# Attention values of the wide tiles by halves, in three of the gates' PSUM banks and beside the next half's scores

## Chip, cores and metric

One core of a Trainium2 chip. The metric is the device time in microseconds of one execution, median of several.

## The reference

Sliding-window causal attention over 8 batches and 8 heads (576 positions, head size 64, window 64), followed by a gated feed-forward layer without biases on the 4608 tokens of 512 features:

```python
rel = pos[:, None] - pos[None, :]
mask = (rel >= 0) & (rel < 64)
scores = np.where(mask, 0.125 * q @ k.T, -1e9)     # per batch and head
attn = softmax(scores) @ v
x = attn.transpose(0, 2, 1, 3).reshape(4608, 512)
out = (np.maximum(x @ w_gate, 0) * (x @ w_val)) @ w_out   # 512 -> 1536 -> 512
```

Inputs and output are float32; the kernel computes its products in float16 with float32 sums.

## The kernel before

The tokens are worked in ten tiles: four of 384 tokens (tiles 0 to 3), then six of 512 (tiles 4 to 9, the wide ones). The stage of tile t does the feed-forward layer of tile t on TensorE, and beside it, woven in, the attention of tile t+1.

The feed-forward part of a wide stage is `hidden` and `output`. `hidden` makes 12 pairs of tiles of 128 hidden features by 512 tokens: four products with w_gate (h0), four with w_val (h1), each group into one PSUM bank of the pool f_ps. ScalarE takes relu of h0 (`relu`, L453) and VectorE multiplies it with h1 (`gate`, L456) into g_sb. `output` then makes four output tiles of 128 tokens, twelve products each (`out_mm`, L482), also in a bank of f_ps; ScalarE copies each out (`out_evac`, L489) and SP stores it. The twelfth product of the first output tile needs the last gate.

The attention part of a wide tile works on two quads of four 64-token windows. `q_st` makes the 64 score products of a quad (L233: keys as weights, 32 rows by 128 columns of the array, 64 columns moving) into two tiles of two banks of the pool a_ps. `q_exp` (ScalarE, L352, four per quad) and `q_mask` (VectorE, L356, four per quad) make the probabilities pw. `t_pv` makes the 128 value products of both quads at once (L371: pw as weights, 128 rows by 32 columns, 65 columns moving: 64 values and the sum of the probabilities). `t_recip` and `t_norm` (VectorE, L386, L391) divide by the sums, and `t_turn` (L396) transposes into xt, the input of the next stage. A bank holds seven 32-token slices of values (BS = 7); the sixteen slices of a tile and four heads lie as 7, 7 and 2, the twos of both head groups in a bank of f_ps, the rest in all four banks of a_ps.

PSUM has eight banks: f_ps four of one bank (tag h: h0, h1, output tiles, and the rest of the values), a_ps two of two banks (scores and values).

The order of instructions is set by a planner, the Weaver. It counts the time of the large products in a clock of its own, and holds a heap of small pieces with due times: before each group of large products (in `output` before each product) it issues the pieces that are due. A piece may advance the clock by what it returns (0.72 for `q_st`, 1.25 for `t_pv`). `ahead(t)` plans the attention of tile t+1 from the clock T at the start of stage t; `plan_wide` sets its pieces. Each engine works through its own queue in the order issued.

The loads of q, k and v, and the copies that spread v to windows that overlap (`v_spread`), are issued by POOL; v is held for two batches, and a load of v waits until the values that last read its slot are made (`v_load`, L191). Transposes of q and k (`qk_trans`, L185) are on VectorE, and `wide_loads` sets their times.

Of the kernel before, what the change touches and what calls it, by code (L numbers as in the profile page):

```python
# [10 lines left out]
FP32 = mybir.dt.float32  # L11
FP16 = mybir.dt.float16
ACT = mybir.ActivationFunctionType
MUL = mybir.AluOpType.mult
# [30 lines left out]
def kernel(  # L45
# [10 lines left out]
    nc = tc.nc  # L56
    B, H, S, D = q.shape
# [8 lines left out]
    G = 4  # L66
# [3 lines left out]
    NS = 4  # L70
    NL = (NT - NS * TT) // WT
# [8 lines left out]
    a_n = ctx.enter_context(tc.tile_pool(name="a_n", bufs=2))  # L80
# [12 lines left out]
    NG = S // 64  # L93
    VW = D + 2
    v16s = [persist.tile([128, NG, H, VW], FP16, name=f"v16_{i}") for i in range(2)]
# [34 lines left out]
    W = Weaver()  # L130
# [4 lines left out]
    def xt_tile(t):  # L135
        if t not in xts:
            xts[t] = x_sb.tile([128, NC, WT], FP16, name="xt")
        return xts[t]
# [75 lines left out]
    def one_bank(name):  # L214
        return f_ps.tile([128, 512], FP32, name=name, tag="h")

    def two_banks(name):
        return a_ps.tile([128, 2, 512], FP32, name=name, tag="a")
# [10 lines left out]
    def st_block(to, g, hh, n, biased=False):  # L229

        b, w = divmod(n, NG)
        rows = slice(32 * g, 32 * g + 32)
        return [lambda dh=dh: nc.tensor.matmul(  # L233
            to, kTs[b % 2][rows, hh, 64 * w:64 * w + 128, dh], qTs[b % 2][rows, hh, 64 * w:64 * w + 64, dh],
            start=(dh == 0 and not biased), stop=(dh == 1), skip_group_check=biased) for dh in range(2)]

    def run_rows(rows):

        for step in zip(*rows):
            for dh in range(2):  # L240
                for block in step:
                    block[dh]()
# [89 lines left out]
    QW = 4  # L332
    WS = 2 * WT // 64
    BS = 512 // VW
    quads = {}
    wides = {}

    def q_window(qd, i):
        return NS * TT // 64 + QW * qd + i

    def q_st(qd):

        halves = [two_banks("st") for _ in range(2)]
        d = quads[qd] = {"st": [halves[g // 2][:, g % 2] for g in range(G)], "p": [None] * G}
        run_rows([[st_block(d["st"][g][:, 256 * hh + 64 * i:256 * hh + 64 * i + 64], g, hh, q_window(qd, i))
                   for hh in range(2) for i in range(QW)] for g in range(G)])
        return 0.72

    def q_exp(qd, g):
        d = quads[qd]  # L350
        d["p"][g] = a_p.tile([128, 2 * QW, 64], FP16, name="pw")
        nc.scalar.activation(d["p"][g].rearrange("p n c -> p (n c)"), d["st"][g], ACT.Exp, scale=scale)  # L352

    def q_mask(qd, g):
        p = quads[qd]["p"][g]
        nc.vector.tensor_tensor(p, p, mask[:, None, :].to_broadcast([128, 2 * QW, 64]), MUL)  # L356

    def t_pv(t):

        d = wides[t] = {"pv": [two_banks("pv") for _ in range(2)], "rest": one_bank("pv"),  # L360
                        "x": a_n.tile([128, 2, WS, 2, D // 2], FP16, name="xw"), "r": a_n.tile([128, 2, WS, 1], FP32, name="rw")}
        for qh in range(2):
            qd = 2 * (t - NS) + qh
            for hh in range(2):
                for i in range(QW):
                    b, vw = divmod(q_window(qd, i), NG)
                    for s in range(2):
                        n = 2 * (QW * qh + i) + s
                        to = d["pv"][hh][:, n // BS, VW * (n % BS):] if n < 2 * BS else d["rest"][:, VW * (2 * hh + n - 2 * BS):]
                        for j in range(G):  # L370
                            nc.tensor.matmul(to[32 * j:32 * j + 32, 0:D + 1],  # L371
                                             quads[qd]["p"][j][:, QW * hh + i, 32 * s:32 * s + 32],
                                             v16s[b % 2][:, vw, G * hh + j, 0:D + 1],
                                             start=True, stop=True, skip_group_check=True)
        return 1.25

    def t_parts(d, hh):

        rest = d["rest"][:, 0:4 * VW].rearrange("p (a s c) -> p a s c", a=2, c=VW)
        return [(d["pv"][hh][:, k, 0:BS * VW].rearrange("p (s c) -> p s c", c=VW), BS * k, BS * k + BS) for k in range(2)] + [  # L380
            (rest[:, hh], 2 * BS, WS)]

    def t_recip(t, hh):
        d = wides[t]
        for pv, s0, s1 in t_parts(d, hh):
            nc.vector.reciprocal(d["r"][:, hh, s0:s1], pv[:, :, D:D + 1])  # L386

    def t_norm(t, hh, k):
        d = wides[t]
        pv, s0, s1 = t_parts(d, hh)[k]  # L390
        nc.vector.tensor_tensor(d["x"][:, hh, s0:s1], pv[:, :, 0:D].rearrange("p s (c e) -> p s e c", e=2),  # L391
                                d["r"][:, hh, s0:s1, :, None].to_broadcast([128, s1 - s0, 2, D // 2]), MUL)

    def t_turn(t, hh):
        dst = xt_tile(t)[:, 2 * hh:2 * hh + 2].rearrange("p e (s c) -> p s e c", c=32)
        nc.vector.transpose(dst, wides[t]["x"][:, hh])  # L396
        if hh == 1:
            normed[0] = t

    def plan_wide(t, TA, TB, P):  # L400
        for qd, T in ((2 * (t - NS), TA), (2 * (t - NS) + 1, TB)):
            W.at(T, lambda qd=qd: q_st(qd))
            for g in range(G):
                W.at(T + 0.8 + 0.55 * g, lambda qd=qd, g=g: q_exp(qd, g))
                W.at(T + 1.35 + 0.55 * g, lambda qd=qd, g=g: q_mask(qd, g))
        W.at(P, lambda: t_pv(t))
        for hh in range(2):
            W.at(P + 0.7 + 3.0 * hh, lambda hh=hh: t_recip(t, hh))
            for i, k in enumerate((2, 0, 1)):
                W.at(P + 1.0 + 3.0 * hh + 0.5 * i, lambda hh=hh, k=k: t_norm(t, hh, k))  # L410
            W.at(P + 2.4 + 3.0 * hh, lambda hh=hh: t_turn(t, hh))

    def plan_batch(b, load, trans):
        for i, (name, hh) in enumerate((n, hh) for n in "kq" for hh in range(2)):
# [115 lines left out]
    with tc.manual_schedule():  # L530
# [78 lines left out]
        def pair(t, TA, TB, P):  # L609
            for u, T in ((2 * t, TA), (2 * t + 1, TB)):  # L610
                W.at(T, lambda u=u: u_st(u))
                plan_exps(T, u)
            W.at(P, lambda: u_pv(2 * t) + u_pv(2 * t + 1))
            for n in range(2):
                u = 2 * t + n
                W.at(P + 0.7 + 1.7 * n, lambda u=u: u_recip(u))
                for hh in range(2):
                    W.at(P + 0.9 + 0.5 * hh + 1.7 * n, lambda u=u, hh=hh: u_norm(u, hh))
                W.at(P + 1.9 + 1.7 * n, lambda u=u: u_turn(u))
# [12 lines left out]
        def wide_loads(t, T):  # L632
            w0 = q_window(2 * (t - NS), 0)
            b = (w0 + 2 * QW - 1) // NG
            us = list(range(UB * b, UB * b + UB)) if w0 <= NG * b else []
            if t == NS:
                us.insert(0, UB * b - 1)
            if w0 <= NG * b:
                plan_batch(b, T - 12.0, (T, T + 1.4, T + 2.8, T + 4.2))
            for u in us:  # L640
                W.at(T - 6.0, lambda u=u: v_load(u))
                W.at(T + 1.0, lambda u=u: v_spread(u, pool))

        def ahead(t):
            T = W.clock
            if t + 1 < NS:
                pair(t + 1, T + 11.0, T + 14.0, T + 17.5)
            elif t + 1 == NS:
                plan_wide(t + 1, T + 9.5, T + 13.0, T + 16.2)
            elif t + 1 < NS + NL:  # L650
                plan_wide(t + 1, T + 12.0, T + 17.0, T + 22.5)
            if NS <= t + 2 < NS + NL:
                wide_loads(t + 2, T + 36.5 if t >= NS else T + 28.5)

        W.at(15.0, lambda: loads(3, 70.0))
        T = 67.0
# [8 lines left out]
        for t in range(2, NS + NL):  # L665
            ready(t)
            ahead(t)
            hidden(t, ((0, widths[t]),))
            (output if t < NS + NL - 1 else output_last)(t)
# [31 lines left out]
```

## Time and profile before

| | |
|---|---|
| median of 5 runs | 324.64 us (324.61 to 325.17) |
| profiled execution | 325.17 us; its span 323.5 us |
| TensorE clock granted, mean | 0.989 of full speed |
| busy: PE, DVE, ACT, POOL | 314.8, 192.5, 127.2, 93.7 us |
| stages of tiles 4 to 8 (start of `hidden` to start of the next) | 33.88, 33.88, 33.90, 33.80, 33.80 us |

PE is the row of TensorE's products, PEld its weight loads, DVE VectorE, ACT ScalarE, POOL GpSimd, SP SyncE. A row of a timeline gives start, duration, engine, line, operation, what is written and read, the shape, and how many instructions are merged. A row of groups gives after the bar the busy time of all, the mean of one in ns, and the idle time of the engine ahead of them with what ended it. Products are pipelined, so that the ends of PE rows are modelled; starts are compared.

### The profile page before, as it was taken

The numbers are of one execution on the slowest core, as the hardware profiler recorded it, in microseconds if no ns is written. First come the engines' busy times: TensorE is split into PE (matmuls) and PEld (weight loads), VectorE is DVE, ScalarE is ACT, GpSimd is POOL, SyncE is SP. The second block draws the span as 40 slices with busy tenths as digits, with TensorE's granted clock in tenths as the row PEclk, the third lists the DMA queues.
The fourth block names the chain that finished last, engine by engine and source line by source line (L and its number), as shares of the span: only waits on it lengthen the run. The fifth ranks groups of instructions, "written<-read, shape, count | busy, mean of one in ns | idle before, by whom it ended". The sixth has DMA issues, their size and how long they took to land.

```text
span 323.5 us, 8919 instructions
## 1 busy us (share of the span) xinstructions
PE 314.8 (97%) x3863; PEld 169.3 (52%) x3863; DVE 192.5 (59%) x369; ACT 127.2 (39%) x250; POOL 93.7 (29%) x138
## 2 busy tenths in 40 slices
PE   6699999999999999999999999999999999999996
PEld 2486958656556644454445444454445444544444
DVE  5947973587938759565765656673767145724410
ACT  3444324534434623542354234613371337223322
POOL 8766335295900290029100920072000000000000
PEclk9789999999999999999999999999999999999999
DMA  8999998979491079009910893092001200020002
GB/s 216 185 196 209 195 105 163 167 141 171 74 187 36 8 102 194 3 5 125 212 13 2 107 199 31 2 104 88 0 2 37 97 0 2 5 108 22 0 34 98
DMA packets 52488, 29.48 MB, mean 91 GB/s; under 512 B 38880, under 2 KB 43872, under 8 KB 52448
## 3 DMA queue, kind: packets, MB, share of 16 engines
q0 software_dynamic: 46688, 18.29, 48.5%
q1 hardware_dynamic: 5616, 10.55, 9.0%
q8 instruction: 30, 0.49, 0.6%
q14 instruction: 10, 0.08, 0.1%
q10 hardware_dynamic: 144, 0.07, 0.1%
HBM read 37.75 MB, written 9.44 MB: 146 GB/s over the span
## 4 chain that ended last, share of the span: by engine, by line
PE 95%; POOL 2%; DMA 2%; issue 0%; ACT 0%; POOLq 0%
PE h L468 59%; PE op L482 28%; PE st L233 3%; PE pv L371 2%; DMA v<-in_v_dram 2%; PE pv L293 1%; PE op L514 1%; POOL v L191 1%; POOL k L167 0%; POOL v L202 0%; POOL v L200 0%; POOL q L167 0%; PE st L207 0%; POOL ident L107 0%; POOL ident L111 0%
## 5 line engine op out<-in xcount | busy, mean ns | idle before, releaser
L456 DVE TENSOR_TENSOR g_sb<-r_sb,h 128x512 f16<-128x512 f32 (+1 forms) x120 | 75.3, 630 | 86.9 <-PE h L468 85.2
L468 PE MATMUL h<-xt,wg 128*128 128x512 f16 (+2 forms) x544 | 113.2, 341 | 0.1
L468 PE MATMUL h<-xt,wv 128*128 128x512 f16 (+2 forms) x544 | 111.3, 336 | 0.0
L453 ACT ACTIVATE r_sb<-h 128x512 f32<-128x512 f32 (+1 forms) x120 | 66.7, 558 | 90.2 <-PE h L468 84.3
L482 PE MATMUL op<-wo,g_sb 128*128 128x512 f16 x420 | 93.9, 380 | 0.0
L468 PEld LDWEIGHTS <-wg 128*128 128x128 f16 x544 | 52.3, 100 | 42.7 <-issue 0.6
L468 PEld LDWEIGHTS <-wv 128*128 128x128 f16 x544 | 50.5, 98 | 40.8
L482 PEld LDWEIGHTS <-g_sb 128*128 128x128 f16 x420 | 40.2, 98 | 47.2
L191 POOL DMA_DIRECT2D v<-in_v_dram x41 | 34.5, 859 | 94.8 <-PE pv L371 90.1
L489 ACT COPY o_sb<-op 128x512 f32<-128x512 f32 x35 | 20.5, 585 | 84.7 <-PE op L482 84.5
L356 DVE TENSOR_TENSOR pw<-pw,mask 128x512 f16<-128x512 f16 x48 | 19.3, 422 | 14.7 <-ACT pw L352 14.3
L352 ACT ACTIVATE pw<-st 128x512 f16<-128x512 f32 x48 | 25.7, 606 | 5.0 <-PE st L233 4.7
L200 POOL COPY v<-v 64x512 f16<-64x512 f16 (+1 forms) x21 | 15.4, 734 | 24.6 <-DMA v<-in_v_dram 23.7
L185 DVE STREAM_TRANSPOSE kT<-k 128x576 f32<-128x576 f32 x16 | 19.9, 1245 | 0.2 <-ACT k L178 0.2
L185 DVE STREAM_TRANSPOSE qT<-q 128x576 f32<-128x576 f32 x16 | 19.3, 1236 | 0.1
L267 ACT ACTIVATE p<-st 128x384 f16<-128x384 f32 (+1 forms) x40 | 14.0, 442 | 8.1 <-PE st L233 8.0
L391 DVE TENSOR_TENSOR xw<-pv,rw 128x448 f16<-128x448 f32 (+1 forms) x36 | 16.2, 507 | 0.4
L202 POOL COPY v<-v 64x512 f16<-64x512 f16 (+1 forms) x21 | 16.0, 764 | 1.0
L233 PEld LDWEIGHTS <-kT 32*128 32x128 f16 x1152 | 10.6, 93 | 10.1 <-issue 7.8
L233 PE MATMUL st<-qT,kT 32*128 32x64 f16 x1152 | 12.7, 190 | 2.9 <-DVE qT L185 2.9
L396 DVE STREAM_TRANSPOSE xt<-xw 128x1024 f16<-128x1024 f16 x12 | 14.9, 1245 | 0.4
L272 DVE TENSOR_TENSOR p<-p,mask 128x384 f16<-128x384 f16 x24 | 9.5, 414 | 3.3 <-ACT p L267 3.1
(45 smaller groups left out, 99.7 us busy)
## 6 DMA issues: line engine op xcount, KB each, us to landing
out_dram<-o_sb SPq DMA_DIRECT2D x35, 256.0 KB, 2.8
k<-in_k_dram POOLq DMA_DIRECT2D x15, 288.0 KB, 5.4
q<-in_q_dram POOLq DMA_DIRECT2D x15, 288.0 KB, 8.1
v<-in_v_dram POOLq DMA_DIRECT2D x31, 128.0 KB, 9.2
wg<-in_moe_w_gate_dram POOLq DMA_DIRECT2D x6, 256.0 KB, 6.5
wv<-in_moe_w_val_dram POOLq DMA_DIRECT2D x6, 256.0 KB, 8.2
wo<-in_moe_w_out_dram POOLq DMA_DIRECT2D x3, 512.0 KB, 12.4
v<-in_v_dram POOLq DMA_DIRECT2D x10, 64.0 KB, 5.9
```

Of the source, the lines that this page charges most:

```text
L185: nc.vector.transpose(dst.rearrange("p (i j) -> p j i", i=32)[:, j0:j1], src[:, j0:j1])
L191: nc.gpsimd.dma_start(v16s[b % 2][lo:hi, g, :, 0:64], v[b, :, 64 * g - 64 + lo:64 * g - 64 + hi].rearrange("h p d -> p h d"))
L202: copy(t[0:64, g0:g1:2, h0:h1, 0:64], t[64:128, g0 - 1:g1 - 1:2, h0:h1, 0:64])
L233: return [lambda dh=dh: nc.tensor.matmul(to, kTs[b % 2][rows, hh, 64 * w:64 * w + 128, dh], qTs[b % 2][rows, hh, 64 * w:64 * w + 64, dh], ...
L352: nc.scalar.activation(d["p"][g].rearrange("p n c -> p (n c)"), d["st"][g], ACT.Exp, scale=scale)
L356: nc.vector.tensor_tensor(p, p, mask[:, None, :].to_broadcast([128, 2 * QW, 64]), MUL)
L391: nc.vector.tensor_tensor(d["x"][:, hh, s0:s1], pv[:, :, 0:D].rearrange("p s (c e) -> p s e c", e=2), d["r"][:, hh, s0:s1, :, None].to_bro ...
L453: nc.scalar.activation(part(r_sb), part(h1), ACT.Relu)
L456: nc.vector.tensor_tensor(g_sb[:, f:f + w, c0:c0 + n], part(r_sb), part(h2), MUL)
L468: nc.tensor.matmul(h[:, b * n:b * n + n], wt[:, c, (f + b) * 128:(f + b) * 128 + 128], xt[:, c, c0:c0 + n], start=(c == 0), stop=(c == NC ...
L482: nc.tensor.matmul(op, g_sb[:, f, bass.ds(sub * 128, 128)], wo[:, f], start=(f == 0), stop=(f == NF - 1))
L489: nc.scalar.copy(o_sb, op)
```

## The change

The values are made by quads (`q_pv`, 64 products) and no longer by tiles. Their two times seven slices and the two odd slices lie in three banks of f_ps, where the gates' and output tiles live; a_ps holds scores alone. Each quad has its own three reciprocals and three normalisations, one for each bank, in the order of the banks; the two transposes follow the second quad.

Each quad's values are planned for the same time as the scores of the following quad (`plan_quad` calls `plan_scores(qd + 1, T)`), so that the scores of a quad are made one quad earlier than before, and the exps and masks of the quads fall into the output stage: the first quad of tile t+1 at T+19.5 (T+21.7 in the stage of tile 6), the second at T+26.5. In the stage of tile 3 the first scores stand alone at T+9.5, and the two quads of tile 4 at T+13.5 and T+18.3. Loads and the times of `wide_loads` are as before.

The diff, the removed `t_pv`, `t_parts`, `t_recip`, `t_norm` and `plan_wide` (shown above) cut:

```diff
+    def q_pv(qd):
+        t, qh = NS + qd // 2, qd % 2
+        if t not in wides:
+            wides[t] = {"x": a_n.tile([128, 2, WS, 2, D // 2], FP16, name="xw"), "r": a_n.tile([128, 2, WS, 1], FP32, name="rw")}
+        d = quads[qd]
+        d["pv"] = [one_bank("pv") for _ in range(3)]
+        for hh in range(2):
+            for i in range(QW):
+                b, vw = divmod(q_window(qd, i), NG)
+                for s in range(2):
+                    n = 2 * i + s
+                    to = d["pv"][hh][:, VW * n:] if n < BS else d["pv"][2][:, VW * hh:]
+                    for j in range(G):
+                        nc.tensor.matmul(to[32 * j:32 * j + 32, 0:D + 1],
+                                         d["p"][j][:, QW * hh + i, 32 * s:32 * s + 32],
+                                         v16s[b % 2][:, vw, G * hh + j, 0:D + 1],
+                                         start=True, stop=True, skip_group_check=True)
+        return 0.6
+
+    def q_part(qd, k):
+        t, s0 = NS + qd // 2, 2 * QW * (qd % 2)
+        pv = quads[qd]["pv"][k]
+        if k < 2:
+            return wides[t], pv[:, 0:BS * VW].rearrange("p (a s c) -> p a s c", a=1, c=VW), slice(k, k + 1), slice(s0, s0 + BS)
+        return wides[t], pv[:, 0:2 * VW].rearrange("p (a s c) -> p a s c", a=2, c=VW), slice(0, 2), slice(s0 + BS, s0 + 2 * QW)
+
+    def q_recip(qd, k):
+        d, pv, a, s = q_part(qd, k)
+        nc.vector.reciprocal(d["r"][:, a, s], pv[:, :, :, D:D + 1])
+
+    def q_norm(qd, k):
+        d, pv, a, s = q_part(qd, k)
+        n = s.stop - s.start
+        if k < 2:
+            nc.vector.tensor_tensor(d["x"][:, k, s], pv[:, 0, :, 0:D].rearrange("p s (c e) -> p s e c", e=2),
+                                    d["r"][:, k, s, :, None].to_broadcast([128, n, 2, D // 2]), MUL)
+        else:
+            nc.vector.tensor_tensor(d["x"][:, :, s.start], pv[:, :, 0, 0:D].rearrange("p a (c e) -> p a e c", e=2),
+                                    d["r"][:, :, s.start, :, None].to_broadcast([128, 2, 2, D // 2]), MUL)
...
+    def plan_scores(qd, T):
+        W.at(T, lambda: q_st(qd))
+        for g in range(G):
+            W.at(T + 0.8 + 0.55 * g, lambda g=g: q_exp(qd, g))
+            W.at(T + 1.35 + 0.55 * g, lambda g=g: q_mask(qd, g))
+
+    def plan_quad(qd, T):
+        W.at(T, lambda: q_pv(qd))
+        for i, k in enumerate((0, 1, 2)):
+            W.at(T + 0.7 + 0.6 * i, lambda k=k: q_recip(qd, k))
+            W.at(T + 0.7 + 0.6 * i, lambda k=k: q_norm(qd, k))
+        if qd % 2 == 1:
+            for hh in range(2):
+                W.at(T + 2.6 + 1.0 * hh, lambda hh=hh: t_turn(NS + qd // 2, hh))
+        if qd + 1 < 2 * NL:
+            plan_scores(qd + 1, T)
...
             elif t + 1 == NS:
-                plan_wide(t + 1, T + 9.5, T + 13.0, T + 16.2)
+                plan_scores(0, T + 9.5)
+                plan_quad(0, T + 13.5)
+                plan_quad(1, T + 18.3)
             elif t + 1 < NS + NL:
-                plan_wide(t + 1, T + 12.0, T + 17.0, T + 22.5)
+                plan_quad(2 * (t + 1 - NS), T + (21.7 if t == NS + 2 else 19.5))
+                plan_quad(2 * (t + 1 - NS) + 1, T + 26.5)
```

More of the change, by code (lines that the diff above doesn't have):

```diff
@@ L356, in q_mask @@
         nc.vector.tensor_tensor(p, p, mask[:, None, :].to_broadcast([128, 2 * QW, 64]), MUL)
[L358 to L392, printed above, removed]
+    def q_pv(qd):
[16 more added lines that the diff above has]
+        return 0.6
@@ L398, in t_turn @@
             normed[0] = t
[L400 to L411, printed above, removed]
+    def plan_scores(qd, T):
[13 more added lines that the diff above has]
+            plan_scores(qd + 1, T)
     def plan_batch(b, load, trans):
```

## The prediction

> **What bounds the kernel now.** I read the page first, then the chain of waits, then the timeline of TensorE around the small products.
>
> ```profile
> PE 314.8 (97%) x3863; PEld 169.3 (52%) x3863; DVE 192.5 (59%) x369; ACT 127.2 (39%) x250; POOL 93.7 (29%) x138
> PE 95%; POOL 2%; DMA 2%; issue 0%; ACT 0%; POOLq 0%
> ```
>
> TensorE (PE) carries the end: 95% of the chain. A busy PE need not be a PE at its peak, so I check its rate. The chain in order of time (start, duration, what) has these pieces:
>
> ```profile
> 187.85 12.09 PE h L468 x56
> 211.68 10.04 PE op L482 x46
> ```
>
> That is 0.216 to 0.218 us for one 512-wide product, and nothing is waited for. So in the wide stages PE neither idles nor waits; only what stands between the large products can be saved. The timeline of PE in the stage that computes tile 4 shows that:
>
> ```profile
> 131.16 1.03 PE L468 MATMUL h<-xt,wv 128*128 128x512 f16 x4
> 132.12 0.68 PE L233 MATMUL st<-qT,kT 32*128 32x64 f16 x64
> 132.73 1.04 PE L468 MATMUL h<-xt,wg 128*128 128x512 f16 x4
> 133.61 1.03 PE L468 MATMUL h<-xt,wv 128*128 128x512 f16 x4
> ...
> 142.10 0.59 PE L482 MATMUL op<-wo,g_sb 128*128 128x512 f16 x2
> 142.62 1.33 PE L371 MATMUL pv<-v,pw 128*32 128x65 f16 x128
> 143.88 0.82 PE L482 MATMUL op<-wo,g_sb 128*128 128x512 f16 x3
> ...
> 79.33 0.55 PE L233 MATMUL st<-qT,kT 32*128 32x64 f16 x48
> 79.82 0.82 PE L468 MATMUL h<-xt,wv 128*128 128x384 f16 x4
> ```
>
> Compare starts, since ends are modelled. Four products take 0.863 us (134.47 to 135.33), so after 131.16 the next is due at 132.02; the scores start at 132.12: **0.10 us to enter a burst**. The 64 scores hold PE for 0.61 us (132.12 to 132.73), 48 for 0.49: 16 more cost 0.12, so 0.0078 us each, and 0.61 less 64 of them leaves **0.11 to 0.12 us to leave a burst**. The 128 values take 1.26 us here and 1.19 us in the last such stage (278.05 to 279.24): 8.9 and 8.4 ns each once 0.12 is taken off; entering costs 0.09 (142.53 due, 142.62).
>
> **What the skill says.** The Trainium skill, "TensorEngine Tiling (Array Packing)", Key Properties, says that changing the tiling mode drains TensorE. The trace agrees that each change of shape (128x128 to 32x128 or to 128x32, and back) costs about 0.1 us; it holds no place in steady work where values (128x32) stand directly beside scores (32x128). "PSUM — Partial Sum Buffer", PSUM bank collisions, says to guard a bank by semaphore as a whole: a bank is a tile's until its last reader has done. No run here shows a collision; that an output tile is read 0.585 us by ScalarE does show.
>
> **The change, part by part.**
>
> *Bursts on PE.* Before: six wide tiles with two score bursts and one of 128 values each, 18 bursts, 36 changes of shape. After: the first scores alone, then eleven times 64 values followed at once by 64 scores, then 64 values alone: 13 bursts, 26 changes at their ends plus 11 between values and scores, 37 in all. The number of products is the same, 768 scores and 768 values. Entering 0.095, leaving 0.117: before 18 x 0.212 = 3.82 us; after 13 x 0.212 = 2.76 us plus 11 inner changes. The inner change is not in the trace. From below it costs 0 (the two modes run into each other): 2.76, a gain of 1.06 us. From above it is a full leaving and entering, 0.212: 5.09, a loss of 1.27 us. I take 0.12, like the leaving of a burst, since what goes before is also a short product and what follows also needs its weights loaded anew: 1.32, together 4.08, **a loss of 0.26 us** over the kernel.
>
> *The gates' banks.* Before, values sat in both pairs of banks of the other pool and in one gate bank; now three of the four gate banks. The first half comes at T+19.5, before the last gate tile of the stage: 23 tiles of 0.8636 plus 0.095 put it at 19.96 us after the stage's start. The banks it takes were read long before: the second-last gate (DVE, ends about 19.9) stands before the third bank, first written 28 values later (20.2). The last value tile then has the fourth bank. The second half falls in the second output tile, after 21 output products: 22.13 + 21 x 0.216 + 0.1 = 26.76. The third output tile starts at 28.7 and takes the first bank released: that of the first normalisation, done near 27.95. Cost 0, with 0.7 us of cover.
>
> *Vector and scalar work.* Counts and sizes per tile stay: 6 reciprocals, 6 normalisations, 8 masks, 2 transposes, 8 exps; they only move. What moves them onto the path is the last gate, which stands behind them in DVE's order and which the twelfth product of the first output tile needs.
>
> ```profile
> L456 DVE TENSOR_TENSOR g_sb<-r_sb,h 128x512 f16<-128x512 f32 x72 | 49.3, 686 | 66.9 <-PE h L468 65.8
> L352 ACT ACTIVATE pw<-st 128x512 f16<-128x512 f32 x48 | 25.7, 606 | 5.0 <-PE st L233 4.7
> L356 DVE TENSOR_TENSOR pw<-pw,mask 128x512 f16<-128x512 f16 x48 | 19.3, 422 | 14.7 <-ACT pw L352 14.3
> L396 DVE STREAM_TRANSPOSE xt<-xw 128x1024 f16<-128x1024 f16 x12 | 14.9, 1245 | 0.4
> 143.67 0.56 DVE L386 RECIPROCAL rw<-pv 128x7 f32<-128x7 f32 x3 [0.61 <-PE pv L371]
> 147.12 1.35 DVE L391 TENSOR_TENSOR xw<-pv,rw 128x128 f16<-128x128 f32 x3
> ```
>
> In a row the following spacings hold: masks 0.335 (three in 1.09), exps 0.485 (four in 2.06), a 448-wide normalisation 0.53 and a 128-wide one 0.21 (three in 1.35). In the stage's own time: values at 19.96, scores from 20.65 to 21.14, first exp 0.25 later, 21.39 to 21.99, the others each 0.485 on, to 23.45. DVE can read the first bank at 20.40; two reciprocals (0.21 each with their wait) and normalisations end at 21.88; first mask at 22.05 (after its exp), then 0.39 for the third bank, masks two and three to 23.46, last gate 23.46 to 24.15. The twelfth output product is due at 22.13 + 11 x 0.216 = 24.50, its weights (0.1 us to load) must be there by 24.39. **Cover 0.2 us; cost 0.** In the stage of tile 6 the burst comes at T+21.7, behind that gate, and this does not arise. Second half: DVE from 27.2, normalisations, four masks waiting on exps (one of them behind the output copy on ACT), two transposes: the last ends at 33.1. The next stage needs xt at 33.9. Cover 0.8 us.
>
> *The narrow stage before.* With 384-wide tiles the second values need the fourth mask (18.2 us after the stage's start) at 18.45, and their third bank needs the last gate (18.7) at 18.7. Cover 0 to 0.2, once.
>
> *POOL, SP and DMAs.* No DMA is added or moved in its queue; SP's 35 output stores keep their order. But the loads of v stand behind the values that last read a slot, and queries, keys and v spreads queue behind them on POOL:
>
> ```profile
> POOL v L191 <- PE pv L371: 90.1, 4, 23.5
> ```
>
> That wait now ends with the second half, some 4 us later (26.8 instead of 22.7 us into the stage), for a slot of that half; where the slot belongs to the first half it ends 3 us earlier. Behind it lie about 7.5 us of POOL work and a landing of 5.4 us (k) to 8.1 us (q). The q and k loaded then are transposed about 40 us after their issue (150.9, 190): hidden with more than 20 us to spare.
>
> **The sum.** 0.26 us on the path, nothing else. Against the profiled execution: span 323.5 becomes 323.8, and 325.17 becomes 325.4; that execution is the slowest of the five, 0.53 above the median, and what lies around its span (1.7 us) does not change. Against the median, 324.64 + 0.26 = 324.9 us.
>
> **Rivals.** *The inner change is nearly free*, because short products drain quickly: at 0 to 0.04 us the kernel gains 1.06 to 0.62, 323.6 to 324.0, faster. For it: the bursts fall from 18 to 13. Against it: leaving after a short product costs no less than entering after a long one (0.117 against 0.095). *The last gate comes late*, slower: five stages less the one at T+21.7 are four places. Nine vector instructions stand between the first half's values and that gate; each 0.07 us slower than I set them and it is 0.6 late, of which 0.2 is covered: four times 0.4, 324.9 + 1.6 = 326.5. It decides from 0.2 us of lateness; over 0.2% from 0.3 us. Against it: the order lets the gate pass ahead of the fourth mask. *The third output tile is given the second one's bank* instead of a freed one: its copy stands behind three exps (29.65 to 30.23) while PE wants the bank at 28.7, 1.6 us in five stages, 333. I take banks to be handed on in order of release, and the normalisation is earlier, so this is unlikely. *PE's bursts do not change the time at all* differs from my forecast by less than a measurement resolves.
>
> **How the numbers follow.** About 0.2%, 0.65 us, is what a measurement of this kernel can tell from no change. My forecast (inner change 0.06 to 0.14 us, covers hold): 0.62, with its own range 324.2 to 325.2. Free inner change: 0.13. Late gate or another short wait: 0.20. Wrong bank: 0.05. So faster 0.13, same 0.62, slower 0.25. The range from 323.9 to 326.4 leaves out the wrong bank, part of the late gate and the very lowest inner cost.
>
> **What would show it.** In the profile after: values and scores standing side by side on PE, 64 and 64; values' start to the scores' start 0.56 + 0.12 us; no idle time between output products beyond 0.216; wide stages of 33.9 us as before. A stall in front of the twelfth output product shows the late gate; one of 1.6 us in front of the third output tile, the wrong bank. Scores starting within 0.6 us of the values' start would prove the inner change free and my sum wrong.

## The result, and the profile after

The median after is 325.29 us (325.03 to 327.49, 24 runs), before 324.68 us (324.37 to 325.55, 44 runs). The ratio is 1.0021, 95% interval 1.0015 to 1.0027: slower by 0.61 us, at the edge of what I had said a measurement can tell from no change. The forecast was 324.9 us, within a range of 323.9 to 326.4; the result lies in that range.

The page after, first its busy times and then its chain of waits by engine:

```profile
PE 315.0 (97%) x3863; PEld 169.9 (52%) x3863; DVE 196.6 (61%) x369; ACT 127.6 (39%) x250; POOL 94.9 (29%) x138
PE 94%; DVE 3%; DMA 1%; ACT 0%; issue 0%; DVEq 0%
```

TensorE still carries the end. New is DVE, with 3% of the chain and 4.1 us more busy time for the same 369 instructions: some of them ran longer.

The span moved by 0.1 us only (323.6), less than the median. In this profiled execution the stage of tile 3, where the change begins, starts at 93.35 us, before at 93.78; over the profiles of this study that start lies between 93.25 and 93.97, whatever the kernel. So I compare from that start on. To the last product it is 226.48 us before and 227.10 after, 0.62 more, which fits the medians. By stages (time from one start of `hidden` to the next, in us, worked out from the starts of the products; the row of stages in the table of the kernel before was taken from times rounded to 0.1 us and differs by up to 0.04):

| stage of tile | 3 | 4 | 5 | 6 | 7 | 8 |
|---|---|---|---|---|---|---|
| before | 26.15 | 33.89 | 33.87 | 33.86 | 33.82 | 33.81 |
| after | 27.38 | 33.84 | 33.83 | 33.85 | 33.82 | 33.30 |

The stages of tiles 4 to 7 hardly moved. One burst of scores went from the stage of tile 8 to that of tile 3; it costs 0.71 us with its entering and leaving before, and 0.52 came off where it left. But stage 3 took 1.23 us more, 0.52 beyond that burst, so most of the loss is there. The timeline of PE after shows a stage without waits first (tile 4), then stage 3:

```profile
140.69 0.72 PE L372 MATMUL pv<-v,pw 128*32 128x65 f16 x64
141.34 0.70 PE L233 MATMUL st<-qT,kT 32*128 32x64 f16 x64
141.97 0.61 PE L480 MATMUL h<-xt,wv 128*128 128x512 f16 x2
...
111.98 1.06 PE L372 MATMUL pv<-v,pw 128*32 128x65 f16 x64
112.98 0.69 PE L233 MATMUL st<-qT,kT 32*128 32x64 f16 x64
113.61 0.60 PE L494 MATMUL op<-wo,g_sb 128*128 128x512 f16 x2
```

In stage 4 values and scores stand side by side: 0.65 us from the first value to the first score, 0.63 to the next large product. In stage 3 the second values take 1.00 us to the scores, 0.35 too long. Why, the chain of the work that ended last shows, in order of time (start, duration, what):

```profile
110.45 0.85 DVE pw L356
...
111.69 0.41 DVE pw L356
112.10 0.47 DVE g_sb L468
112.58 0.04 issue
112.62 0.43 PE pv L372 x31
```

The timelines of DVE and POOL in the same stretch, with the whole length of each instruction:

```profile
110.25 0.29 DVE L397 TENSOR_TENSOR xw<-pv,rw 128x128 f16<-128x128 f32 x1
110.45 0.85 DVE L356 TENSOR_TENSOR pw<-pw,mask 128x512 f16<-128x512 f16 x1
111.23 0.54 DVE L468 TENSOR_TENSOR g_sb<-r_sb,h 128x384 f16<-128x384 f32 x1
111.69 0.41 DVE L356 TENSOR_TENSOR pw<-pw,mask 128x512 f16<-128x512 f16 x1
112.03 0.54 DVE L468 TENSOR_TENSOR g_sb<-r_sb,h 128x384 f16<-128x384 f32 x1
```

```profile
109.72 1.31 POOL L200 COPY v<-v 64x1024 f16<-64x1024 f16 x1
111.08 0.69 POOL L202 COPY v<-v 64x512 f16<-64x512 f16 x1
```

The chain runs from the third mask through the fourth and the last gate to the values, and two products of this burst start late. The fourth product reads the probabilities of the fourth mask: that mask ends at 112.10, and the product starts at 112.16, 0.17 us after the third. The 33rd is the first in the burst's second bank, and the wait ends with the gate at 112.57: it starts at 112.62, 0.24 us after the 32nd. In stage 4 the same two steps take less than 0.01 and 0.02 us. (The forecast and the expectations below call this bank the third; the values of the third bank, from the 29th product on, start without a wait.) The third mask, ahead of both, took 0.85 us, double, while GpSimd copied v at the same time. Before, those copies began at 112.79 (below), when no mask was left to do:

```profile
112.79 1.04 POOL L200 COPY v<-v 64x1024 f16<-64x1024 f16 x1
```

The masks as a whole (durations least/median/longest, ns), after and then before:

```profile
L356 DVE TENSOR_TENSOR pw<-pw,mask x48: 375/419/990, 104.6 to 280.1; 128x512 f16<-128x512 f16 x48
```

```profile
L356 DVE TENSOR_TENSOR pw<-pw,mask x48: 417/422/427, 105.0 to 275.6; 128x512 f16<-128x512 f16 x48
```

Before, no mask of the wide tiles met a copy of v on GpSimd, and none exceeded 427 ns. After, seven took 826 to 990 ns. Each of these began while such a copy was under way and ended 0.28 us after it. Overlap alone is not what counts: the mask that began at 109.70, just before the copy of 109.72, kept its 0.43 us, and that copy took 1.31 us where the one of 112.79 before took 1.04. Masks that began in the last 0.15 us of a copy lost nothing either. This agrees with what the Trainium skill, "SBUF — State Buffer", Who interferes with whom, states: a VectorE instruction with two SBUF inputs contends with a GpSimd instruction that reads SBUF. The mask product has two SBUF inputs; the gate and the normalisation read one operand from PSUM and kept their length (0.54 and 0.62 us).

The profile before held the sign already. Of the 24 masks of the narrow tiles (L272), 21 took 0.36 us at most; three that came up in the midst of a copy of v took 0.70 to 1.03 us and ended 0.21 us after that copy. The longest, from the timelines of DVE and POOL before:

```profile
83.66 1.03 DVE L272 TENSOR_TENSOR p<-p,mask 128x384 f16<-128x384 f16 x1 [0.27 <-ACT p L267]
83.44 1.04 POOL L202 COPY v<-v 64x1024 f16<-64x1024 f16 x1
```

A second wait in stage 3: the last value tile of `hidden` starts 0.18 us late (110.59), until the third bank of the first values is read (the normalisation of L397 above ends at 110.54). A third of 0.08 us stands in stage 8: the last values have no scores behind them, so the third output tile comes that much sooner and has to wait until the first normalisation frees a bank (it ends at 284.12, the product starts at 284.18). Together 0.35 + 0.18 + 0.08 = 0.61 us.

### The profile page after: what moved, and what is told of

The parts are those of the page before. It is cut to its first block, busy times and chain, and to the rows that moved or that the text cites. A ratio compares the mean times of both kernels' runs of the same rounds, so it can differ in the third digit from the quotient of the medians.

```text
span 323.6 us, 8930 instructions
## 1 busy us (share of the span) xinstructions
PE 315.0 (97%) x3863; PEld 169.9 (52%) x3863; DVE 196.6 (61%) x369; ACT 127.6 (39%) x250; POOL 94.9 (29%) x138
## 4 chain that ended last, share of the span: by engine, by line
PE 94%; DVE 3%; DMA 1%; ACT 0%; issue 0%; DVEq 0%
PE h L480 58%; PE op L494 28%; PE st L233 3%; PE pv L372 2%; PE pv L293 2%; DMA k<-in_k_dram 1%; PE op L526 1%; DVE qT L185 1%; DVE kT L185 1%; DVE pw L356 1%; DVE xw L394 0%; DVE g_sb L468 0%; ACT k L178 0%; DVE q L178 0%; PE st L207 0%
## 5 line engine op out<-in xcount | busy, mean ns | idle before, releaser
L200 POOL COPY v<-v 64x512 f16<-64x512 f16 (+1 forms) x21 | 16.1, 766 | 23.7 <-DMA v<-in_v_dram 22.9
L356 DVE TENSOR_TENSOR pw<-pw,mask 128x512 f16<-128x512 f16 x48 | 22.1, 481 | 1.3 <-ACT pw L352 1.2
L202 POOL COPY v<-v 64x512 f16<-64x512 f16 (+1 forms) x21 | 16.5, 785 | 1.0
L388 DVE RECIPROCAL rw<-pv 128x7 f32<-128x7 f32 (+1 forms) x36 | 6.8, 188 | 14.6 <-PE pv L372 14.6
L394 DVE TENSOR_TENSOR xw<-pv,rw 128x448 f16<-128x448 f32 x24 | 15.0, 624 | 0.8
```

Source lines behind the costliest of these rows:

```text
L200: copy(t[64:128, g0:g1:2, h0:h1, 0:64], t[0:64, g0 + 1:g1 + 1:2, h0:h1, 0:64])
L202: copy(t[0:64, g0:g1:2, h0:h1, 0:64], t[64:128, g0 - 1:g1 - 1:2, h0:h1, 0:64])
```

## Experiments

My theory after the result: the shape changes on TensorE nearly even out, and the loss is these waits, the longest brought about by a mask that met a GpSimd copy. The rival: the loss is the price of the changes of shape, and the waits would only fill time lost anyway. All ratios are to the kernel before, with the 95% interval.

**later_quad** plans the second values of tile 4 later, behind the gate.

```diff
-                plan_quad(1, T + 18.3)
+                plan_quad(1, T + 19.4)
```

> The second values of tile 4 are planned 1.1 us later (T+19.4 in place of T+18.3) in the stage of tile 3. If the loss over before is mostly the wait of those values for their third bank (the gate behind a mask that ran twice as long), the 64 values take 0.52 us in place of 0.87 us and the time falls by 0.35 us, to 324.9 us (ratio to before 1.0008). If the loss is all in changes of shape on TensorE, the time stays at 325.3 us (1.0019).

Measured 324.96 us (ratio 1.0009, 1.0001 to 1.0017), 0.33 less than after. The 64 values took 0.516 us. The mask still took 0.85 us; nobody waited for it any more. So the wait was worth its length in the total, against the rival.

**kq_first** leaves every plan of PE, ACT and DVE and only makes GpSimd copy later in stage 3.

```diff
                 plan_quad(1, T + 18.3)
+                for name in "kq":
+                    for hh in range(2):
+                        W.at(T + 29.2, lambda name=name, hh=hh: qk_load(5, name, hh))
...
-                plan_batch(b, T - 12.0, (T, T + 1.4, T + 2.8, T + 4.2))
+                plan_batch(b, None if t == NS + 2 else T - 12.0, (T, T + 1.4, T + 2.8, T + 4.2))
```

> The four loads of q and k of the next batch are issued on GpSimd ahead of the v copies in the stage of tile 3, so that these copies start about 2.2 us later and no longer meet the third mask of the second quad; plans on all other engines are as after the change. If that mask was held up by the GpSimd copy, it takes 0.42 us in place of 0.85 us, the last gate ends 0.43 us earlier, the second values take 0.52 us in place of 0.87 us, and the time falls by 0.35 us to 324.9 us. If the gate is late by the order of VectorE's work alone, the mask keeps 0.85 us or the values their 0.87 us, and the time stays at 325.3 us.

Measured 324.94 us (ratio 1.0012, 0.9997 to 1.0028): 0.35 less than after. One run of 327.94 makes the interval wide enough to hold the 1.0021 of after; but eleven of the 13 runs took 325.11 us or less, and of the 24 after only one did. The timelines of POOL, DVE and PE of this run:

```profile
111.98 1.04 POOL L200 COPY v<-v 64x1024 f16<-64x1024 f16 x1
```

```profile
110.56 0.41 DVE L356 TENSOR_TENSOR pw<-pw,mask 128x512 f16<-128x512 f16 x1
110.89 0.54 DVE L468 TENSOR_TENSOR g_sb<-r_sb,h 128x384 f16<-128x384 f32 x1
111.36 0.42 DVE L356 TENSOR_TENSOR pw<-pw,mask 128x512 f16<-128x512 f16 x1
111.69 0.55 DVE L468 TENSOR_TENSOR g_sb<-r_sb,h 128x384 f16<-128x384 f32 x1
```

```profile
112.09 0.72 PE L372 MATMUL pv<-v,pw 128*32 128x65 f16 x64
112.74 0.70 PE L233 MATMUL st<-qT,kT 32*128 32x64 f16 x64
```

With the copy out of its way the mask is back at 0.41 us, the last gate ends at 112.24 (0.44 us earlier, counted from the start of the stage), and the values take 0.65 us to the scores again. VectorE's order is the same; moving the copy was enough to bring mask and gate back. Two later masks met the shifted copies in this run, and no one waited for them.

**third_first** takes the second wait by itself: the third bank is read ahead of the second mask.

```diff
-            W.at(T + 0.7 + 0.6 * i, lambda k=k: q_recip(qd, k))
-            W.at(T + 0.7 + 0.6 * i, lambda k=k: q_norm(qd, k))
+            W.at(T + 0.7 + 0.55 * i, lambda k=k: q_recip(qd, k))
+            W.at(T + 0.7 + 0.55 * i, lambda k=k: q_norm(qd, k))
```

> Reciprocal and normalisation of the third bank are planned 0.1 us earlier, so that they stand ahead of the second mask on VectorE. In the stage of tile 3 the last value tile's first product should then no longer be 0.18 us late for that bank: the time falls by 0.1 to 0.2 us, to 325.1 us; the wait in the second values stays (0.87 us for the 64). If that late product costs nothing, the time stays at 325.3 us.

Measured 325.83 us (ratio 1.0036, 1.0023 to 1.0048): 0.54 slower than after, and I had expected it faster. The late product is gone, but DVE and PE in stage 3 show what came instead:

```profile
110.03 1.67 DVE L356 TENSOR_TENSOR pw<-pw,mask 128x512 f16<-128x512 f16 x2
```

```profile
112.22 1.23 PE L372 MATMUL pv<-v,pw 128*32 128x65 f16 x64 [0.42 <-DVE g_sb L468]
113.38 0.69 PE L233 MATMUL st<-qT,kT 32*128 32x64 f16 x64
```

The second mask, moved behind the third bank, now met a copy as well: two masks in a row took 1.67 us, where two that meet no copy take 0.76 (those of 105.81 before). The values entered 0.49 us late and then ran 0.52 us long: 1.0 us lost where after lost 0.35, against 0.18 gained, 0.47 of the 0.54 that the medians show. Had I looked where the copies lie, I would have seen it coming.

**both** joins third_first with the later second values.

> Both edits: the second values of tile 4 at T+19.4 and the third bank's reciprocal and normalisation ahead of the second mask. If the two waits are all that stands between the sum of the bursts and the result, 0.53 us goes: 324.75 us, within 0.1 us of before (ratio 1.0002 to 1.0005). If changes of shape make up the loss of 0.6 us, 325.2 us or more is left.

Measured 324.80 us (ratio 1.0001, 0.9993 to 1.0009), as expected. Both masks still ran double; with the values later that cost nothing.

**apart** prices the change of shape by splitting values from scores.

```diff
-            plan_scores(qd + 1, T)
+            plan_scores(qd + 1, T + 1.5)
```

> The kernel after the change, with the scores planned 1.5 us after the values of the same quad, so that large products lie between them: eleven changes of shape from values to scores become a leaving and an entering each. With the forecast's prices (0.212 less 0.12) that adds 1.0 us: 326.3 us, if no wait comes or goes. If a direct change from values to scores were nearly free, it would add 11 times 0.2 us, 2.2 us: 327.5 us. If direct changes cost as much as leaving and entering, nothing is added: 325.3 us.

Measured 328.69 us (ratio 1.0131, 1.0101 to 1.0162), above all that I had written. The total says little, since new waits came: values in stage 3 waited 1.4 us for masks planned later, and 0.48 in stage 6. The burst table tells the price apart from them. Where values and scores touch, the last value's start and the first score's lie 0.133 us apart; split, the last value to the next large product again takes 0.133 us (or more, where that product waits), and the scores pay 0.096 on top to enter. Eleven times that is 1.05 us of the 3.4 us; the values' waits are another 1.5, and about 0.9 are waits for a bank. In five places the large product behind the values starts 0.11 to 0.14 us late. In four of them it is the last value tile of `hidden`, which takes over a bank when the relu before it ends, as in stage 4 (ACT, then PE):

```profile
142.58 0.60 ACT L465 ACTIVATE r_sb<-h 128x512 f32<-128x512 f32 x1 [1.13 <-PE h L480]
143.23 1.02 PE L480 MATMUL h<-xt,wv 128*128 128x512 f16 x4
```

And the third output tile's 0.08 us, seen after in stage 8 alone, now stands in five stages. After, the scores filled that time: with three of the four gate banks full of values, they are what keeps PE busy until a bank is free.

**before_split** asks the same of the kernel before: 128 values as 64 and 64.

```diff
-        W.at(P, lambda: t_pv(t))
+        W.at(P - 1.2, lambda: t_pv(t, 0))
+        W.at(P, lambda: t_pv(t, 1))
```

The lines by which `t_pv` makes one half at a call are cut.

> The kernel before, with the 128 values of a wide tile in two bursts of 64 (the first before the last value tile of hidden, the second at the start of output), in the same banks as before; six more bursts. At 0.212 us for entering and leaving that adds 1.27 us; if 64 values in one burst take 0.516 us and 128 take 1.05 to 1.13 us, as the profiles of before and after show, 0.06 us comes back six times: 0.9 us in all, 325.6 us. If the count of shape changes costs nothing, 324.7 us.

Measured 326.68 us (ratio 1.0052, 1.0034 to 1.0070), 1.1 us above the expectation. PE in stage 3 and in stage 4 of this run:

```profile
108.63 0.42 PE L373 MATMUL pv<-v,pw 128*32 128x65 f16 x32
109.86 0.43 PE L373 MATMUL pv<-v,pw 128*32 128x65 f16 x32 [0.80 <-ACT pw L352]
...
142.09 0.69 PE L373 MATMUL pv<-v,pw 128*32 128x65 f16 x64
142.71 1.04 PE L471 MATMUL h<-xt,wv 128*128 128x512 f16 x4
143.68 0.72 PE L373 MATMUL pv<-v,pw 128*32 128x65 f16 x64
```

In stage 3 the first half came too early and waited 0.96 us for its probabilities: that is the excess. In the stages of tiles 4 to 8 the price of one burst more is clean: 34.00 us each against 33.81 to 33.89 before, 0.11 to 0.19 us. That is 0.22 for entering and leaving, less what two runs of 64 values save over one of 128. The estimate of 0.15 net stands.

**six_early** puts the stage of tile 6 at T+19.5 like the others.

```diff
-                plan_quad(2 * (t + 1 - NS), T + (21.7 if t == NS + 2 else 19.5))
+                plan_quad(2 * (t + 1 - NS), T + 19.5)
```

> The kernel after the change, with the first half of tile 7 at T+19.5 as in the other stages in place of T+21.7. If covers are as in the other stages (last gate 0.2 to 0.3 us early for the twelfth output product), nothing changes: 325.3 us. If in this stage GpSimd copies meet the masks ahead of the last gate, that gate is 0.4 us late once and the time rises by 0.1 to 0.4 us: 325.4 to 325.7 us.

Measured 325.35 us (ratio 1.0017, 1.0008 to 1.0027), no difference from after. Stage 6 took 33.85 us as with T+21.7; the gate's cover holds there too (it ends at 212.39, the twelfth output product starts at 212.78).

**clear_all** takes all three waits away: the edits of kq_first and third_first, and the last half of all earlier.

```diff
-                plan_quad(2 * (t + 1 - NS) + 1, T + 26.5)
+                plan_quad(2 * (t + 1 - NS) + 1, T + (25.6 if t + 2 == NS + NL else 26.5))
```

> The change with its three waits taken away: loads of q and k ahead of the v copies on GpSimd in the stage of tile 3, third bank ahead of the second mask, and the last half of all at T+25.6. In the stage of tile 3 the copies no longer meet the masks, so that the third bank's place costs no gate here. If waits and bursts are all there is, 0.61 us goes and the time is 324.7 us, within 0.1 us of before (ratio 0.9997 to 1.0004): the change itself neither gains nor loses. If the added shape changes cost 0.26 us net, as forecast, 324.95 us.

Measured 324.77 us (ratio 0.9999, 0.9990 to 1.0008); from the start of stage 3 to the last product 226.56 us against 226.48 before. A wait of 0.08 us is left in the second values of stage 3, for the last gate. So without its waits the change neither gains nor loses what can be measured, and no version here beats the kernel before.

## Why the prediction was right or wrong

**PE at its limit, nothing but shape changes to save: right.** Stages 4 to 7 moved by 0.05 us at most.

**The bursts.** The gaps at entering (0.093 to 0.095), leaving (0.125) and between values and scores (0.133) sum to 3.99 us in the 18 bursts before and 4.30 in the 13 after, 0.31 more; forecast 0.26. (Behind values, leaving is 0.130 to 0.133.) The inner change, taken at 0.12 from leaving, came to 0.125 once the 0.008 of one product is taken off. That it is nearly free fell: values' start to scores' start is 0.65 us, not under 0.6. What I left out: 64 values run faster than half of 128 (0.516 us where 128 take 1.05 to 1.13), 0.36 us over the kernel, against 0.11 that the scores run longer. The bursts net 0.05 us, not 0.26: the one term of my sum was mis-sized, and away from the result. Why a long burst is slower is open: of 128 values the first 64 took 0.50 us and the others 0.55 to 0.63.

**"Cover 0 to 0.2, once": this step failed.** It is the narrow stage. I had a bank due at the moment when the last gate ends, the fourth mask 0.25 us ahead of need, and counted 0. Both were late, 0.35 us together, and the bank was the second one and not the third; the bank of the first values came to 0.18 more, a wait I had not listed. The timing of that gate held within 0.1 us but for one thing, the doubled mask, 0.43 us. I had written that the wait of the v loads ends 3 us earlier where the slot belongs to a first half, and looked only at who waits for what comes behind it, not at what it runs beside. The 0.18 came from the order of two pieces due at the same time: the mask went first.

**The last gate in the wide stages: right.** In stage 4 it ended at 144.83, where the twelfth output product's weights were due at 145.1; stages 5, 7 and 8 show the same 0.3 us. In stage 4 a mask that meets a copy, at 144.74, stands just behind this gate; ahead of it, its extra 0.42 us would have been more than the cover. **The wrong bank: did not occur**; but the third output tile's 0.08 us in stage 8 was missed. **xt: it cost nothing, but the 0.8 us of cover did not hold.** In stage 4 the last transpose ended 0.96 us ahead of the next stage. With two masks of the second half doubled it was 0.11 us in stage 5; in stage 6 the transpose ended at 222.29, and the next stage had begun at 222.26, which its first two products, that read the earlier half, covered.

So that the total came out slower, 0.61 us against 0.26, was largely luck. The price of the bursts on which the forecast rested is 0.05 us of it; nearly all the rest are waits that I had counted at nothing. (Bursts and waits add up to 0.66 us, 0.04 more than the 0.62 measured from the start of stage 3; what offsets them I do not know.)

## What to carry to other kernels

When a change makes a transfer or copy start earlier, look at what runs beside it then: here VectorE's product of two SBUF tensors, 0.42 us alone, took 0.83 to 0.99 us seven times because it came up while GpSimd was copying. Where it matters, move the copy or the VectorE work, as kq_first and later_quad did. On a saturated TensorE, count changes of array shape, not bursts: values beside scores saved the 0.09 us of entering and not the 0.125 of leaving. And a cover smaller than what one such meeting costs (0.2 us against 0.43 here) holds only as long as nothing meets; move the piece, or give its wait a price.

## What the runs showed that I had not expected

The lengthened masks are alike in all runs: every wide mask that took more than 0.43 us had begun during a copy of v and ended 0.27 to 0.28 us after it, as if it had waited for the copy to end; one that had begun first kept its length. So what such a meeting costs depends on what is left of the copy: 0.08 us (a mask of 0.50 in kq_first) to 0.69 us (one of 1.11 in apart).

And the scores behind the values do more than spare a change of shape: they give VectorE and ScalarE the time to free a bank. It shows where they are missing: in stage 8, and all through **apart**.
